# Attention, MoE 1 and MoE 2 on one core: wider staging of MoE 1's weights, nine subtractions moved to VectorE, and new start addresses for split operands

## The chip, the core and the metric

The kernel runs on one core of a Trainium2 chip. A core has TensorE (PE, with its weight loads shown apart as PEld), VectorE (DVE), ScalarE (ACT), GpSimd (POOL) and SyncE (SP), each with its own instruction queue that runs in order, and 16 DMA engines. The metric is the device time of one execution in microseconds; smaller is better.

## The reference

```python
def _attn_ref(q, k, v):                       # (4, 8, 576, 64)
    scores = scale * np.matmul(q, k.transpose(0, 1, 3, 2))
    mask = block_i >= block_j                 # blocks of 64
    scores = np.where(mask, scores, -1000000000.0)
    ...
    return np.matmul(attn, v)                 # softmax in between

def _moe_ref(x, w1, w2, w3, w_out):           # 2304 tokens, 512 -> 1024 -> 512
    a = x @ w1
    b = x @ w2
    h = a * b @ w3
    return h @ w_out

def _moe2_ref(x, w_gate, w_noise, noise, w1, w2):   # 8 experts, top 2
    logits = x @ w_gate
    noisy_logits = logits + np.log1p(np.exp(x @ w_noise)) * noise
    ...
    for e in range(E):
        ...
            h = np.maximum(x[mask] @ w1[e], 0.0)
            out[mask] += top2_w[mask, k, None] * (h @ w2[e])
```

The attention's output, put together over the heads, is the input x of the first MoE, whose output is the input of the second.

## The kernel before

Nearly all products are made of three matmuls (`mm3`, L485 to L487): each operand is split into a high part and a low part in a 32-bit format (`split`, L476 and L480: ACT copies the high part, DVE or POOL subtracts it for the low part), and high x high, high x low and low x high are added up in PSUM. A matmul has a stationary operand, loaded by PEld, and a moving one that streams through the array.

**Attention.** 32 heads (4 batches of 8) run one after the other. Per head, `prep_h` (L604) makes `hi` on ACT (L607, L610), the low half of q on DVE (L609) and `kl`, k's low part, on POOL (L612). `s_unit` multiplies (L639, L642), `s_max` takes the row maxima on DVE (L653) and the exponentials on ACT (L658), `g_unit` transposes (L672) into `pt`, `av_a` and `av_b` multiply with v (L685, L697). The order in which these steps, the conversions and the fillers are recorded is written out by hand in two lists, `FIRST` (L70, for the heads up to number 9) and `LATER` (L71): g, p, a, b, s, h, v and l are steps of heads, `c` is `feed`, `t` a step of the router, `f` lets filler work for PE in. A scheduler then moves instructions within each engine's queue.

**MoE 1's weights.** They arrive as 64-bit numbers. `load64` (L536) fetches a piece of 512 numbers per partition (512 KB in all) into `stg`, which has two buffers; `conv64` (L541) makes 32-bit numbers of it in `stf` with three DVE instructions (L547 to L549), and `feed_half` (L764) splits the piece of the call before into `pc` (L476 on ACT, L480 on DVE), converts the next and issues the load of the one two further on. There are 40 pieces (`w_jobs`, L734). The piece's buffers lie in a pool that stays open as long as the attention.

**MoE 1.** `w_unit` (L717) first multiplies w3 by w_out (64 units of three matmuls, 512 columns wide), so that MoE 1 becomes (x w1 * x w2) w3w_out. After batch 0's heads, `Moe1.steps` (L370) goes over 9 chunks of 256 tokens: `x_load` (L154) fetches the heads' outputs, which were written to DRAM as `x2`, `x_prep` (L185) normalizes and splits them into `x.h` (tile `xh`, L195), `ab` (L199, 8 times a chunk) multiplies 24 times with `xh` as the moving operand, 256 columns, and a piece of w1 or w2 in `pc` as the stationary one; the products' split goes to `gt` (L212). `yout` (L215) multiplies 48 times a chunk with `gt` stationary and `pc` moving, 512 columns. `ab` for unit f waits at recording for the conversions: 28 + 4 * (f // 2) pieces have to be split before. The router (L254) follows each chunk in small steps and keeps its transposed input in `yT`.

**MoE 2.** Per expert, `trans` (L930) makes `xt0` (three blocks of 128 tokens) and `xt1` (two blocks); `ffn1` (L944) multiplies 96 times with `xt` moving (384 columns for `xt0`, 256 for `xt1`) and `pc` stationary; its split goes to `ht0` and `ht1`. `ffn2` (L959) multiplies 24 times for each of the 40 blocks with `ht` stationary and `pc` moving, 512 columns.

## Time and profile before

| | us |
|---|---|
| median of 3 runs | 1100.47 (1100.3 to 1101.81) |
| the profiled execution | 1103.1 |
| its span, first to last instruction | 1101.2 |
| PE busy | 1050.4 |
| DVE busy | 564.4 |
| ACT busy | 494.9 |
| POOL busy | 309.3 |

The profile is of one execution. Busy time counts overlapping instructions of an engine once. A matmul's recorded duration is longer than the distance to the next one, since matmuls are pipelined; what a matmul costs in a row of equal ones is the distance between their starts. The granted TensorE clock (PEclk) is a share of 2.4 GHz and is either 1.0 or 0.5 at any moment; a stretch's figure is the mean.

### The profile page before, as it was taken

The numbers are of one execution on the slowest core, as the hardware profiler recorded it, in microseconds if no ns is written. First come the engines' busy times: TensorE is split into PE (matmuls) and PEld (weight loads), VectorE is DVE, ScalarE is ACT, GpSimd is POOL, SyncE is SP. The second block draws the span as 40 slices with busy tenths as digits, with TensorE's granted clock in tenths as the row PEclk, the third lists the DMA queues.
The fourth block names the chain that finished last, engine by engine and source line by source line (L and its number), as shares of the span: only waits on it lengthen the run. The fifth ranks groups of instructions, "written<-read, shape, count | busy, mean of one in ns | idle before, by whom it ended". The sixth has DMA issues, their size and how long they took to land.

```text
span 1101.2 us, 17515 instructions
## 1 busy us (share of the span) xinstructions
PE 1050.4 (95%) x6588; PEld 941.2 (85%) x6588; DVE 564.4 (51%) x1270; ACT 494.9 (45%) x1180; POOL 309.3 (28%) x315
## 2 busy tenths in 40 slices
PE   4999978999999999999999999999999999999996
PEld 3767767799899999989999889889898989899885
DVE  5988889856665756532454453534333333434111
ACT  5765547666665656422223432433333333333111
POOL 3110122424252242422443325241413222120211
PEclk9999989999999999999999999999999999999999
DMA  9765775325634463322413556563545445351212
GB/s 218 237 199 193 196 200 180 123 79 132 196 96 105 143 156 121 107 68 59 77 40 87 126 106 184 173 163 96 148 102 144 107 125 125 106 115 30 39 20 32
DMA packets 80386, 136.34 MB, mean 124 GB/s; under 512 B 21437, under 2 KB 46757, under 8 KB 80293
## 3 DMA queue, kind: packets, MB, share of 16 engines
q1 hardware_dynamic: 70181, 113.98, 36.4%
q0 software_dynamic: 10112, 21.16, 10.7%
q8 instruction: 54, 0.88, 0.3%
q14 instruction: 39, 0.32, 0.1%
HBM read 103.92 MB, written 31.19 MB: 123 GB/s over the span
## 4 chain that ended last, share of the span: by engine, by line
PE 81%; DMA 8%; DVE 7%; ACT 1%; issue 1%; SPq 1%; POOL 0%; POOLq 0%; DVEq 0%; ACTq 0%
PE ph L485 13%; PE ph L486 13%; PE ph L487 13%; PE m L485 9%; PE m L486 9%; PE m L487 9%; DMA stg<-in_w_dram 4%; PE tp L672 4%; PE av L697 3%; PE sb L642 2%; PE sb L639 2%; PE m L939 1%; DVE stf L549 1%; DVE nm L653 1%; DMA stf<-in_m_dram 1%
## 5 line engine op out<-in xcount | busy, mean ns | idle before, releaser
L485 PE MATMUL m<-xh,pc 128*128 128x256 f32 x576 | 165.2, 290 | 5.6 <-DVE at L211 3.5
L486 PE MATMUL m<-xh,pc 128*128 128x256 f32 x576 | 163.1, 287 | 2.2 <-DVE xh L480 2.2
L487 PE MATMUL m<-xh,pc 128*128 128x256 f32 x576 | 161.2, 287 | 1.9 <-DVE pc L480 1.9
L485 PE MATMUL ph<-xt,pc 128*128 128x384 f32 (+1 forms) x512 | 156.0, 308 | 2.9 <-ACT xt L476 1.6
L486 PE MATMUL ph<-xt,pc 128*128 128x384 f32 (+1 forms) x512 | 157.0, 307 | 0.0
L487 PE MATMUL ph<-xt,pc 128*128 128x384 f32 (+1 forms) x512 | 156.9, 307 | 0.0
L954 DVE SCALAR_TENSOR_TENSOR ht<-ph,ht 128x384 fp32r<-128x384 f32 (+1 forms) x128 | 61.6, 489 | 148.7 <-ACT ht L953 143.5
L480 DVE TENSOR_TENSOR pc<-stf,pc 128x1024 fp32r<-128x1024 f32 (+1 forms) x92 | 92.3, 1016 | 87.2 <-ACT pc L476 83.8
L485 PE MATMUL ph<-pc,ht 128*128 128x512 f32 x320 | 127.8, 400 | 0.0
L486 PE MATMUL ph<-pc,ht 128*128 128x512 f32 x320 | 126.5, 396 | 0.0
L487 PE MATMUL ph<-pc,ht 128*128 128x512 f32 x320 | 126.4, 395 | 0.0
L981 POOL DMA_INDIRECT out_dram<-yo,ids x40 | 64.3, 1606 | 211.5 <-ACT yo L977 124.0
L485 PEld LDWEIGHTS m<-xh,pc 128*128 128x128 f32 x576 | 110.5, 193 | 7.2 <-DVE at L211 3.7
L953 ACT ACTIVATE ht<-ph 128x384 fp32r<-128x384 f32 (+1 forms) x128 | 55.0, 437 | 133.8 <-PE ph L487 127.1
L486 PEld LDWEIGHTS m<-xh,pc 128*128 128x128 f32 x576 | 110.3, 193 | 3.0 <-DVE xh L480 2.6
L487 PEld LDWEIGHTS m<-xh,pc 128*128 128x128 f32 x576 | 109.0, 192 | 2.7 <-DVE pc L480 2.4
L476 ACT CAST pc<-stf 128x1024 fp32r<-128x1024 f32 (+1 forms) x92 | 78.1, 864 | 73.8 <-DVE stf L549 32.5
L658 ACT ACTIVATE pb<-sb,nm 128x288 f32<-128x288 f32 (+3 forms) x192 | 93.5, 496 | 38.4 <-PE tp L672 17.3
L480 POOL TENSOR_TENSOR gt<-at,gt 128x256 fp32r<-128x256 f32 x72 | 57.2, 798 | 183.9 <-ACT gt L476 175.7
L485 PEld LDWEIGHTS ph<-xt,pc 128*128 128x128 f32 x512 | 95.7, 188 | 4.0 <-ACT xt L476 2.1
L612 POOL TENSOR_TENSOR kl<-qk,hi 128x576 fp32r<-128x576 f32 x32 | 47.5, 1484 | 177.2 <-ACT hi L610 136.6
L486 PEld LDWEIGHTS ph<-xt,pc 128*128 128x128 f32 x512 | 96.2, 188 | 0.6 <-DVE xt L480 0.2
(158 smaller groups left out, 2229.0 us busy)
## 6 DMA issues: line engine op xcount, KB each, us to landing
stf<-in_m_dram SPq DMA_DIRECT2D x52, 512.0 KB
qk<-in_qk_dram SPq DMA_DIRECT2D x32, 576.0 KB
stg<-in_w_dram SPq DMA_DIRECT2D x32, 512.0 KB
x<-ev SPq DMA_DIRECT2D x32, 288.0 KB
xab<-x SPq DMA_DIRECT2D x20, 256.0 KB
yt<-y SPq DMA_DIRECT2D x18, 260.0 KB
stg<-in_w_out_dram SPq DMA_DIRECT2D x8, 512.0 KB
v<-in_v_dram SPq DMA_DIRECT2D x24, 160.0 KB
```

The source lines that it names most:

```text
L476: d = nc.scalar.copy(h, src)
L480: return d, eng.tensor_tensor(l, src, r32(h), op=OP.subtract)
L485: nc.tensor.matmul(out, a, c, start=first, stop=False)
L486: nc.tensor.matmul(out, a, d, start=False, stop=False)
L487: nc.tensor.matmul(out, b, c, start=False, stop=last)
L612: nc.gpsimd.tensor_tensor(c.kl, c.qk[:, 1, :], r32(c.hi[:, 1, :]), op=OP.subtract)
L658: nc.scalar.activation(pb[t][:, k0:k0 + src.free_size()], src, AF.Exp, bias=nm, scale=1.0, accum_out=sums[:, h // H, t + n, h % H:h % H + 1])
L672: nc.tensor.transpose(bank[:, n * P:(n + 1) * P], pb[t][:, kt * P:(kt + 1) * P], self.ident)
L697: nc.tensor.matmul(c.av[:, o0:o0 + w], c.vv[:, kt, :], c.pt[:, i, s0:s0 + w], start=(kt == 0 and i == 0), stop=(kt == 4 and i == m - 1))
L953: a = nc.scalar.activation(hh[:, 0, f, :], ph, AF.Relu)
L954: v = nc.vector.scalar_tensor_tensor(hh[:, 1, f, :], ph, 0.0, r32(hh[:, 0, f, :]), op0=OP.max, op1=OP.subtract)
L981: nc.gpsimd.indirect_dma_start(out=self.a["out"], out_offset=self.idx(e, i), in_=yo, in_offset=None, compute_op=OP.add)
```

## The change

1. **Weights in wider pieces.** `stg` and `stf` become 1024 numbers wide, `stg` with two buffers as before and `stf` with one in place of two. `w_jobs` yields 6 pieces of 512 and 17 of 1024 where there were 40 of 512, and `FIRST` has three `c` where it had five. The pool of `stg` and `stf` closes once all pieces are split, and `yT` is put into a pool opened after that.
2. **kl on VectorE.** For heads 0 to 8 the subtraction that makes `kl` is done by DVE; heads 9 to 31 stay on POOL.
3. **Places in SBUF.** The first heads' `pt` lies in the right-hand pool; the first of `gt`'s eight buffers is allocated as soon as its pool opens; `xh` gets 16 numbers (64 bytes) ahead of it; `xt1`'s tile gets 112 numbers behind it; `wv` gets names by the expert's parity in place of two buffers.

Where the tiles begin follows from the two built programs. In bytes of a partition, modulo 512:

| tile | before | after | its part in the matmuls |
|---|---|---|---|
| xh | 384 | 448 | moving, `ab` |
| pc, all 12 | 128 | 128 | stationary in `ab` and `ffn1`, moving in `yout` and `ffn2` |
| gt | 384 | 384 | stationary, `yout` |
| ht0 | 416 | 384 | stationary, `ffn2` |
| ht1 | 448 | 384 | stationary, `ffn2` |
| xt0 | 352 | 352 | moving, `ffn1` |
| xt1 | 448 | 448 | moving, `ffn1` |
| pt, heads 8 to 31 | 480 | 320 | moving, `av` |
| yT | 384 | 448 | moving, router |

Every slice that a matmul takes of these tiles lies a multiple of 512 bytes further on, but for `pt`, where some lie 256 further.

```diff
-FIRST = "g0 g1 t f2.9 c t c o g2 g3 t p s0 t t s1 s2 f2.9 c t a f2.9 t b0 t s3 h t t c c b1 v l"
+FIRST = "g0 g1 t f2.9 c t o g2 g3 t p s0 t t s1 s2 f2.9 c t a f2.9 t b0 t s3 h t t c b1 v l"
...
-            x.h = self.p2b.tile([P, 2, 4, CH], F32R, name="xh")
+            x.h = self.p2b.tile([P, 16 + 8 * CH], F32R, name="xh")[:, 16:].rearrange("p (a t c) -> p a t c", a=2, t=4)
...
-        gt = self.gts[c, f] = self.p2b.tile([P, 2, CH], F32R, name="gt", bufs=8)
+        gt = self.gts[c, f] = self.gt0 if (c, f) == (0, 0) else self.new_gt()
...
-            self.yT = self.p2b.tile([P, 2, 4, CH], F32R, name="yT")
+            self.yT = self.p2c.tile([P, 2, 4, CH], F32R, name="yT")
...
     def load64(self, src, n):
-        t = self.stg.tile([P, 512], I64, name="stg")
+        w = n * src.shape[-1]
+        t = self.stg.tile([P, 1024], I64, name="stg", bufs=2)[:, 0:w]
...
-        f = self.stg.tile([P, 512], F32, name="stf")
+        f = self.stg.tile([P, 1024], F32, name="stf")[:, 0:wi.shape[1]]
...
-                nc.gpsimd.tensor_tensor(c.kl, c.qk[:, 1, :], r32(c.hi[:, 1, :]), op=OP.subtract)
+                (nc.vector if h < NF - 1 else nc.gpsimd).tensor_tensor(c.kl, c.qk[:, 1, :], r32(c.hi[:, 1, :]), op=OP.subtract)
...
-                        c.pt = px.tile([P, 1, PTW], F32, name="pt", bufs=2)
+                        c.pt = pt0[:, h % 2:h % 2 + 1, :]
...
                 for half in range(2):
                     for ft in range(2):
                         yield w3(ft, half * 512)
-                    for g in range(4 * half, 4 * half + 4):
-                        yield wout(g)
+                    if half == 0:
+                        for g in range(2):
+                            yield wout(g)
+                    for g in range(2 + 2 * half, 4 + 4 * half, 2):
+                        yield wout2(g)
                 for ft in range(2, 8):
-                    for o in (0, 512):
-                        yield w3(ft, o)
+                    yield w3(ft, 0, 1024)
                 for m, (n, k, i) in enumerate(W12):
-                    for o in (0, 2):
-                        yield a[n][:, o:o + 2, k * 256:(k + 1) * 256], 2, i, o * 256, 0 if m < 2 else 64
+                    yield a[n][:, :, k * 256:(k + 1) * 256], 4, i, 0, 0 if m < 2 else 64
...
+                if i >= H and moe1.p2c is None and moe1.conv == 40:
+                    stgs.close()
+                    moe1.p2c = moe1.p2s.enter_context(tc.tile_pool(name="p2c", bufs=1, reuse_waits="tile"))
...
-        x = self.xt[e, s] = (self.pa if s == 0 else self.pb).tile([P, 2, 4, n * P], F32R, name=f"xt{s}")
-        wv = self.wv[e, s] = self.pa.tile([P, n], F32, name=f"wv{s}", bufs=2)
+        x = (self.pa if s == 0 else self.pb).tile([P, 8 * n * P + 112 * s], F32R, name=f"xt{s}")
+        x = self.xt[e, s] = x[:, 0:8 * n * P].rearrange("p (m d c) -> p m d c", m=2, d=4)
+        wv = self.wv[e, s] = self.pa.tile([P, n], F32, name=f"wv{s}{e % 2}")
```

VectorE's queue around the eighth head's preparation (`hi` is that head's; `stf` and `stg` are pieces of weights, `nm` row maxima, `ev` a head's output, `tp` and `sb` banks of PSUM). Before:

```order
L547 TENSOR_SCALAR stf_441<-stg_360 128x512
L653 TENSOR_REDUCE nm4_1056<-sb_1050 128x1
L687 COPY ev_1029<-tp_1027 128x128
L548 SCALAR_TENSOR_TENSOR stf_441<-stg_360,stf_441 128x512
L656 TENSOR_REDUCE nm4_1056<-nm4_1056 128x1
L609 SCALAR_TENSOR_TENSOR hi_1186<-qk_1089,hi_1186 64x576
L547 TENSOR_SCALAR stf_449<-stg_401 128x512
L549 SCALAR_TENSOR_TENSOR stf_441<-stg_360,stf_441 128x512
L548 SCALAR_TENSOR_TENSOR stf_449<-stg_401,stf_449 128x512
L653 TENSOR_REDUCE nm0_1137<-sb_1131 128x1
L653 TENSOR_REDUCE nm1_1139<-sb_1131 128x1
L549 SCALAR_TENSOR_TENSOR stf_449<-stg_401,stf_449 128x512
```

With the change:

```order
L553 SCALAR_TENSOR_TENSOR stf_361<-stg_285,stf_361 128x1024
L554 SCALAR_TENSOR_TENSOR stf_361<-stg_285,stf_361 128x1024
L661 TENSOR_REDUCE nm4_941<-sb_935 128x1
L484 TENSOR_TENSOR pc3_70<-stf_361,pc3_70 128x1024
L661 TENSOR_REDUCE nm0_1011<-sb_1005 128x1
L664 TENSOR_REDUCE nm4_941<-nm4_941 128x1
L661 TENSOR_REDUCE nm1_1013<-sb_1005 128x1
L695 COPY ev_910<-tp_908 128x128
L617 SCALAR_TENSOR_TENSOR hi_1069<-qk_966,hi_1069 64x576
L620 TENSOR_TENSOR kl_1073<-qk_966,hi_1069 128x576
L552 TENSOR_SCALAR stf_453<-stg_330 128x1024
L553 SCALAR_TENSOR_TENSOR stf_453<-stg_330,stf_453 128x1024
```

Before, three instructions of pieces 512 wide stand next to the head's `hi` and no `kl`; now `kl` follows `hi` directly, and the two conversions ahead of `hi` are 1024 wide, with the next piece right behind `kl`.

SyncE's queue where chunk 0's x is fetched (`ev` is head 7's output on its way to DRAM, `x2`; `xab` is x's tile; names in brackets are the semaphores it waits for: DMAHW0 to 7 are earlier DMAs, PE the matmuls). Before:

```order
L538 DMA stg_908<-in_w1_dram 128x2x256 [waits DMAHW6_49,DVE_49]
L538 DMA stg_953<-in_w2_dram 128x2x256 [waits DMAHW7_49,DVE_49]
L701 DMA x2_61<-ev_1408 128x576 [waits DMAHW0_49,Activation_49]
L167 DMA xab_1502<-x2_61 64x3x256 [waits DMAHW1_49,PE_49]
L167 DMA xab_1502<-x2_61 64x3x256 [waits DMAHW2_49]
L172 DMA xr_1503<-rs_62 64x3x256 [waits DMAHW3_49,PE_49]
L167 DMA xab_1502<-x2_61 64x3x256 [waits DMAHW4_49]
L167 DMA xab_1502<-x2_61 64x3x256 [waits DMAHW5_49]
L538 DMA stg_961<-in_w2_dram 128x2x256 [waits DMAHW6_49,DVE_49]
```

With the change:

```order
L543 DMA stg_842<-in_w2_dram 128x4x256 [waits DMAHW5_49,DVE_49]
L709 DMA x2_61<-ev_1265 128x576 [waits DMAHW6_49,DVE_49,Activation_49]
L168 DMA xab_1364<-x2_61 64x3x256 [waits DMAHW7_49,DMAHW6_49,PE_49]
L168 DMA xab_1364<-x2_61 64x3x256 [waits DMAHW0_49]
L173 DMA xr_1365<-rs_62 64x3x256 [waits DMAHW1_49]
L168 DMA xab_1364<-x2_61 64x3x256 [waits DMAHW2_49]
L168 DMA xab_1364<-x2_61 64x3x256 [waits DMAHW3_49]
L173 DMA xr_1365<-rs_62 64x3x256 [waits DMAHW4_49]
L543 DMA stg_906<-in_w1_dram 128x4x256 [waits DMAHW5_49,DVE_49]
```

Before, the first read into `xab` waits for its ring and for PE; now it waits also for DMAHW6, which is the write of `ev` just ahead of it, because `xab` lies over the tile that `ev` had.

## Rows read from the trace of the kernel before

**Rows 1.** Part 1 of the page: busy time, share of the span, instructions.

```profile
PE 1050.4 (95%) x6588; PEld 941.2 (85%) x6588; DVE 564.4 (51%) x1270; ACT 494.9 (45%) x1180; POOL 309.3 (28%) x315
```

**Rows 2.** Stretches: us, busy by engine, granted clock, DMA share, GB/s.

```profile
25.00:84.00 59.00, 55.66 (x295) 41.00 (x294) 52.71 (x102) 42.51 (x116) 8.15 (x6) 0.97 0.70 219
84.00:125.00 41.00, 40.20 (x211) 31.79 (x210) 35.64 (x73) 23.04 (x59) 2.85 (x2) 1.00 0.61 202
125.00:160.00 35.00, 27.53 (x172) 24.31 (x171) 27.24 (x51) 17.43 (x46) 7.29 (x6) 0.90 0.79 193
160.00:207.00 47.00, 38.47 (x247) 33.57 (x246) 44.96 (x83) 30.59 (x85) 16.25 (x13) 0.89 0.51 167
...
300.00:470.00 170.00, 169.78 (x1256) 158.84 (x1255) 106.04 (x303) 101.46 (x295) 62.45 (x62) 1.00 0.44 121
...
720.00:1080.00 360.00, 360.00 (x2046) 323.95 (x2045) 114.21 (x168) 118.94 (x197) 83.45 (x79) 1.00 0.42 100
```

**Rows 3.** Timeline of PE: start, duration; first and last matmul of three rows.

```profile
590.60 0.28 PE L485 MATMUL m<-xh,pc 128*128 128x256 f32 x1
...
593.36 0.28 PE L485 MATMUL m<-xh,pc 128*128 128x256 f32 x1
...
821.03 0.28 PE L485 MATMUL ph<-xt,pc 128*128 128x256 f32 x1
...
831.80 0.28 PE L487 MATMUL ph<-xt,pc 128*128 128x256 f32 x1
...
1068.77 0.28 PE L485 MATMUL ph<-xt,pc 128*128 128x256 f32 x1
...
1079.96 0.28 PE L487 MATMUL ph<-xt,pc 128*128 128x256 f32 x1
```

**Rows 4.** Timeline of PE: first and last of a `yout` and of three `ffn2`.

```profile
498.56 0.40 PE L485 MATMUL m<-pc,gt 128*128 128x512 f32 x1
...
509.24 0.40 PE L487 MATMUL m<-pc,gt 128*128 128x512 f32 x1
...
1051.97 0.40 PE L485 MATMUL ph<-pc,ht 128*128 128x512 f32 x1
...
1068.53 0.40 PE L487 MATMUL ph<-pc,ht 128*128 128x512 f32 x1
```

**Rows 5.** Tile stf up to 208 us: count, ns minimum/median/maximum, first and last start.

```profile
L547 DVE TENSOR_SCALAR stf<-stg x40: 406/424/1544, 7.8 to 203.8; 128x512 int32<-128x512 int32 x40
L548 DVE SCALAR_TENSOR_TENSOR stf<-stg,stf x40: 671/683/1874, 9.3 to 205.7; 128x512 int32<-128x512 int32 x40
L480 DVE TENSOR_TENSOR pc<-stf,pc x39: 620/682/2533, 12.2 to 205.1; 128x512 fp32r<-128x512 f32 x39
```

**Rows 6.** DVE's groups by shape: busy us, mean ns, idle before; last row 625:1080.

```profile
L548 DVE SCALAR_TENSOR_TENSOR stf<-stg,stf 128x512 int32<-128x512 int32 x40 | 31.2, 780 | 0.4
...
L480 DVE TENSOR_TENSOR pc<-stf,pc 128x512 fp32r<-128x512 f32 x39 | 29.1, 749 | 0.4 <-ACT pc L476 0.2
L547 DVE TENSOR_SCALAR stf<-stg 128x512 int32<-128x512 int32 x40 | 20.6, 515 | 17.7 <-DMA stg<-in_w_dram 14.9 <-DMA stg<-in_w_out_dram 2.7
L609 DVE SCALAR_TENSOR_TENSOR hi<-qk,hi 64x576 fp32r<-64x576 f32 x15 | 15.2, 1015 | 6.3 <-ACT hi L607 5.8
...
L480 DVE TENSOR_TENSOR pc<-stf,pc 128x1024 fp32r<-128x1024 f32 x52 | 62.5, 1223 | 86.8 <-ACT pc L476 83.7 <-PE ph L487 3.1
```

**Rows 7.** Line 609 up to 208 us: count, ns minimum/median/maximum; who waited for it.

```profile
L609 DVE SCALAR_TENSOR_TENSOR hi<-qk,hi x15: 755/756/1733, 7.0 to 201.5; 64x576 fp32r<-64x576 f32 x15
...
  PE sb L639: 12.9, 4
```

**Rows 8.** POOL's groups up to 208 us, as Rows 6.

```profile
L612 POOL TENSOR_TENSOR kl<-qk,hi 128x576 fp32r<-128x576 f32 x15 | 22.6, 1509 | 106.9 <-ACT hi L610 104.1 <-PE av L697 2.8
L620 POOL TENSOR_TENSOR vv<-v,vv 128x320 fp32r<-128x320 f32 x6 | 7.2, 1200 | 7.8 <-ACT vv L619 7.7
```

**Rows 9.** The chain that ended last, 100 to 210 us: start, us, what.

```profile
145.02 9.55 DMA stg<-in_w_dram
```

More of the change, by code (lines that the diff above doesn't have):

```diff
@@ L555, in attention @@
         moe1 = self.moe1
-        with tc.tile_pool(name="p1", bufs=1, side="right") as p1, tc.tile_pool(name="stg", bufs=2, side="right") as self.stg, \
+        stgs = ExitStack()
+        with tc.tile_pool(name="p1", bufs=1, side="right") as p1, \
                 tc.tile_pool(name="psS", bufs=3, space=PSUM) as psS, \
@@ L566, in attention @@
             sums = p1.tile([P, B, 6, H], F32, name="sums")
+            pt0 = p1.tile([P, 2, PTW], F32, name="pt")
+            self.stg = stgs.enter_context(tc.tile_pool(name="stg", bufs=1, side="right"))
             hd = {}
```

21 lines of the change are left out of this document (14 added, 7 removed).

## The prediction

> **What bounds the kernel now.** I read the page's busy times first, then a table of stretches, then single instructions. PE is busy 1050.4 of 1101.2 us and has 95% of the span; no other engine reaches 52% [rows 1]. The table of stretches says where PE is the limit and where it isn't [rows 2]. From 300 to 470 us PE is busy 169.78 of 170 us while DVE works 106.04; from 720 to 1080 us it is busy 360.00 of 360. There only fewer or shorter matmuls save time. Before 207 us it is otherwise. From 125 to 207 us (two rows) PE is busy 27.53 + 38.47 = 66.0 of 82 us, at a mean granted clock of 0.90 and 0.89, while DVE works 27.24 + 44.96 = 72.2 of 82: here DVE and what feeds it set the pace. From 25 to 125 us PE and DVE are both near full: PE idles 3.3 + 0.8 us, DVE is busy 88.4 of 100. So PE idles 4.1 + 16.0 = 20.1 us from 25 to 207 us. The clock is at half of 2.4 GHz for about 6% of 59, 20% of 35 and 22% of 47 us, some 21 us in all, which costs up to 10 us more. About 30 us can be won in that part at the very most.
>
> The third reading is the distance between starts of matmuls that follow each other without a break, at a granted clock of 1.0. In `ab` 24 matmuls of 256 columns take (593.36 - 590.60) / 23 = 120.0 ns each. In `ffn1` on `xt1`, with as many columns and the same `pc` as stationary operand, 96 take (831.80 - 821.03) / 95 = 113.4 ns in one expert, and (1079.96 - 1068.77) / 95 = 117.8 ns in another [rows 3]. In `yout` 48 matmuls of 512 columns take (509.24 - 498.56) / 47 = 227.2 ns; in `ffn2`, with the same moving tiles and the same width, 72 take (1068.53 - 1051.97) / 71 = 233.2 ns [rows 4]. At 2.4 GHz the columns alone would be 106.7 and 213.3 ns, so each kind pays its own surplus. What differs within each pair is where the split operand begins: `xh` at 384 modulo 512 against `xt1` at 448; `ht0` at 416 (and `ht1` at 448) against `gt` at 384. The change gives `xh` the place of the faster `xt1` and `ht0`, `ht1` that of the faster `gt`.
>
> **The change part by part: places.** `ab` has 9 chunks x 8 x 24 = 1728 matmuls. If they run as `xt1` does, each saves between 120.0 - 117.8 = 2.2 and 120.0 - 113.4 = 6.6 ns: 3.8 to 11.4 us. No row says into which of the two rates a chain of 24 falls, so I take the middle, 4.4 ns and **7.6 us**. Lower bound nothing, if the place isn't the cause. A loss isn't excluded by a row, but the pair that differs in place alone points the other way, and I give it nothing. `ffn2` has 40 x 24 = 960 matmuls; at 227.2 in place of 233.2 ns they save 960 x 6.0 = **5.8 us** (bounds 0 and 5.8). Nearly all of both lie where PE has no idle time [rows 2], so they count in full. `xt0` and `xt1` begin where they did: nothing. `pt` moves from 480 to 320 beside an unmoved `vv`, and `yT` from 384 to 448; for neither is there a row at the new place, and both are few against the 1728: nothing, and 1 us either way in the range. The names of `wv`, the early `gt` buffer and the pools move no work.
>
> The rule that speaks against this: the Trainium skill, "TensorE: Matmul & The Clock Gate", section "Back-to-back issue gap", gives the distance of two matmuls at the full clock as columns / 2.4 + 2.5 ns, with no word on addresses. It would make 109.2 ns of 256 columns wherever they lie; the trace has 113.4, 117.8 and 120.0 for them, so something beside the width counts. By the rule the moves would be worth nothing, which is the first rival below.
>
> **Wider pieces.** A piece of 512 costs DVE 424 (L547), 683 (L548; L549 is of the same form) and 682 ns (L480) at the median [rows 5], 424 + 683 + 683 + 682 = 2472 ns. The split at 1024 takes 1223 ns [rows 6], so 512 numbers more cost 541 ns and the fixed part is some 140 ns. For L548 and L549 the same slope gives 1224. L547 at 424 ns is below that slope already; with half of it, 271 ns, it comes to 695. A wide piece is then 695 + 1224 + 1224 + 1223 = 4366 ns against 2 x 2472 = 4944: 0.58 us less, and 17 x 0.58 = **9.8 us** of DVE. If L547 doubled instead, 17 x 0.42 = 7.2.
>
> **kl on DVE.** This adds nine subtractions 576 long; the nearest row is L609, also 576 long, at 756 ns undisturbed [rows 7]: 9 x 0.756 = 6.8 us of DVE. It takes nine of the 15 from POOL, 9 x 1.509 = 13.6 us of POOL work [rows 8]. While POOL works, DVE's instructions are stretched: L547's mean is 515 against a median of 424, L548's 780 against 683, L480's 749 against 682, L609's 1015 against 756, with single ones up to 2533 [rows 5 to 7]. Mean less median, times the counts, is 3.6 + 3.9 + 2.6 + 3.9 = 14.0 us. POOL's two largest groups in that time are 22.6 (`kl`) and 7.2 us (`vv`) [rows 8]; of these 29.8 the nine have 46%, of all of POOL's work less, and I take 36%: 5 us of stretch goes. Bounds 0, and 13.6 if every moment of them stood in DVE's way. DVE thus gains 9.8 + 5 - 6.8 = 8 us net. Behind `kl` on DVE's queue now stand the next piece's conversion and row maxima; the head's L642 on PE waits for it.
>
> **Fewer, larger loads.** DVE idles 17.7 us ahead of L547 for a piece to land [rows 6], and the chain has a single wait of 9.55 us for such a load [rows 9]. With two buffers a load starts when the conversion two pieces earlier ends. A wide conversion alone covers 695 + 2 x 1224 = 3.1 us where a narrow one covers 1.8, and half as many hand-overs are left; the bytes are the same and the DMA engines are 51 to 79% busy [rows 2]. I let two thirds of the idle time go, 12 us. One buffer for `stf` costs nothing, since the split that frees it stands ahead of the next conversion on the same queue, as the order shows.
>
> **What of it reaches the end.** DVE wins 8 + 12 = 20 us before 207 us. From 25 to 125 us PE has only 4.1 us to give; from 125 to 207 us it idles 16 us and loses clock besides. I count half of the 20: **10 us**, with bounds of -6 (the queue rival below, weakened) and 20. Chunk 0's x now waits for the write of head 7's `ev`: the read that follows could start earlier before. That is one DMA's landing, between nothing and the 9.55 us of the longest wait [rows 9]; since the write was issued just ahead in both orders, and the last quarter of the reads needs it anyway, I take 2 us and leave it inside the 10's bounds.
>
> The sum: 7.6 + 5.8 + 10 = 23.4 us. From the profiled execution's 1103.1 that leaves 1079.7; the median of the runs is 2.6 lower, and from 1100.47 it leaves **1077**.
>
> **The rivals.** (1) Places don't matter; what differs between `ab` and `ffn1` is their neighbours in the queue and in PSUM. Then the 10 us of the first part are all: 1090. (The rule of the Trainium skill's page above would say the same.) For it: `xt1` itself shows two rates at one place. Against: `ab` keeps 120.0 ns at 590 us, when attention has ended. (2) The first part gains nothing, because PE there waits on latencies that a wide piece lengthens as much as it shortens the sum; the places act: 1100.5 - 13.4 = 1087. For it: PE is 98% busy from 84 to 125 us. Against: 16 us of idle PE after that. (3) Slower: DVE's queue. PE waited 12.9 us, four times, for L609 [rows 7]. A head's `hi` and `kl` now stand behind pieces that hold DVE for 4366 ns in place of 2472, and `kl` itself adds 756. If each of the first 12 heads were late by that difference, 1.9 + 0.8 = 2.7 us, PE would lose 32 us; less the 13.4 of the places that is 1119. It decides from 1.1 us a head on, where the loss eats the places' gain. Against: DVE would have to be full at every head, and its load falls. (4) Both act more strongly: 113.4 ns everywhere (11.4), 5.8, and 16 of the 20 us: 33 us, 1067. That the starts aren't where they should be is no rival, since the built program shows them.
>
> **How the numbers follow.** The forecast, 1070 to 1084, has 0.52. Rival 1 (1085 to 1094) 0.14, rival 2 (1084 to 1091) 0.14, rival 4 (1062 to 1070) 0.08, no change because gains and losses meet 0.05, rival 3 0.07. The range reaches from 1066 to 1093 and leaves out the far halves of rivals 1 and 4, no change, and rival 3. A measurement of this kernel can tell 0.2%, 2.2 us, from no change. Faster by more than that: 0.52 + 0.14 + 0.14 + 0.08 = 0.88; the same 0.05; slower 0.07.
>
> **What would show it.** Places: in the timeline late in MoE 1 the starts in `ab` stand 113 to 118 ns apart where they stood 120.0; in `ffn2` 227 in place of 233; `ffn1` and `yout` as they were. Wider pieces: L548's counterpart at 1024 near 1.22 us, 17 times, and less than 6 us of DVE idle for loads. kl: POOL's groups lose nine of them, DVE has nine near 0.76 us, and the means of the conversions come down to their medians. First part: the last conversion ends some 10 us before 207, and PE's idle time from 125 us to there falls below 10 us. The prediction is wrong if `ab` stays at 120 ns or goes above it, or if PE waits longer for a head's `hi` and `kl` than 12.9 us.

## The result, and the profile after

The changed kernel takes 1092.21 us (median; 1087.97 to 1096.28), the kernel before beside it 1101.29. The ratio is 0.9911, 95% interval 0.9892 to 0.9931: 9 to 10 us faster where 23.4 were forecast. Measured again beside other kernels it was 0.9909 (0.9883 to 0.9935). The direction held and the size did not. The time lies inside the forecast's range, 1066 to 1093, by less than 1 us at its upper end, and the wide range is what held it. The profiled execution took 1091.95 us, its span is 1090.1 and the mean granted clock 0.984 (0.988 before).

Part 1 of the page of the changed kernel, the line that answers [rows 1]:

```profile
PE 1042.4 (96%) x6588; PEld 940.8 (86%) x6588; DVE 566.3 (52%) x1211; ACT 494.6 (45%) x1163; POOL 300.5 (28%) x306
```

PE lost 8 us of busy time, and 11.1 us of the span went. So only some 3 us of PE's idle time is gone. The table of stretches of the changed kernel, as [rows 2], says the same of the first part:

```profile
25.00:84.00 59.00, 54.61 (x305) 42.90 (x306) 54.09 (x96) 45.51 (x124) 0.87 (x1) 0.97 0.78 267
84.00:125.00 41.00, 41.00 (x216) 33.08 (x215) 35.57 (x50) 22.39 (x51) 1.88 (x1) 1.00 0.52 173
125.00:160.00 35.00, 27.29 (x165) 23.50 (x163) 26.70 (x39) 17.16 (x46) 10.94 (x8) 0.85 0.78 203
160.00:207.00 47.00, 38.91 (x239) 34.64 (x240) 44.16 (x67) 28.67 (x75) 15.20 (x11) 0.85 0.48 152
...
720.00:1080.00 360.00, 360.00 (x2066) 327.55 (x2063) 111.76 (x164) 118.53 (x197) 82.48 (x79) 1.00 0.40 96
```

From 125 to 207 us PE is busy 27.29 + 38.91 = 66.2 us, where it was 66.0 [rows 2], and the clock is lower (0.85 against 0.90 and 0.89). In the one stretch in which PE had time to give, nothing was won in this execution.

The places acted. The timeline of PE in the changed kernel (start, duration), as [rows 3, 4]: the first and the last of the same 24 matmuls of `ab`, and of the 72 of `ffn2`:

```profile
586.03 0.28 PE L489 MATMUL m<-xh,pc 128*128 128x256 f32 x1
...
588.74 0.28 PE L489 MATMUL m<-xh,pc 128*128 128x256 f32 x1
...
1041.58 0.39 PE L489 MATMUL ph<-pc,ht 128*128 128x512 f32 x1
...
1057.68 0.39 PE L491 MATMUL ph<-pc,ht 128*128 128x512 f32 x1
```

`ab` stands at (588.74 - 586.03) / 23 = 117.8 ns where it stood at 120.0, and `ffn2` at (1057.68 - 1041.58) / 71 = 226.8 where it stood at 233.2.

Where the time went, read from the starts of six matmuls in the two traces (us from the start of the span; the last column is the gain up to there):

```
                               before    changed    gained
last unit of the w3 product     134.3     128.5       5.8
first ab                        136.3     132.8       3.5
first ab of chunk 1             228.1     226.6       1.5
first ab of chunk 5             470.1     464.8       5.3
first ffn2                      642.6     638.1       4.5
last matmul                    1091.0    1079.9      11.1
```

The first part was ahead by 5.8 us at 129 us and by 1.5 us at 227. `ab` and what stands among it brings 3 us up to `ffn2`, and `ffn2` 6.6.

### The profile page after: what moved, and what is told of

The parts are those of the page before. It is cut to its first block, busy times and chain, and to the rows that moved or that the text cites. A ratio compares the mean times of both kernels' runs of the same rounds, so it can differ in the third digit from the quotient of the medians.

```text
span 1090.1 us, 17403 instructions
## 1 busy us (share of the span) xinstructions
PE 1042.4 (96%) x6588; PEld 940.8 (86%) x6588; DVE 566.3 (52%) x1211; ACT 494.6 (45%) x1163; POOL 300.5 (28%) x306
## 4 chain that ended last, share of the span: by engine, by line
PE 78%; DVE 5%; ACT 1%; DMA 1%; issue 1%; POOL 0%; POOLq 0%; ACTq 0%; DVEq 0%
PE ph L489 13%; PE ph L490 13%; PE ph L491 13%; PE m L489 9%; PE m L490 9%; PE m L491 9%; PE tp L680 3%; PE av L705 3%; PE sb L650 2%; PE sb L647 2%; PE m L957 1%; DMA stf<-in_m_dram 1%; DVE hi L617 1%; PE m L247 1%; DVE stf L553 1%
## 5 line engine op out<-in xcount | busy, mean ns | idle before, releaser
L484 DVE TENSOR_TENSOR pc<-stf,pc 128x1024 fp32r<-128x1024 f32 (+1 forms) x75 | 88.1, 1190 | 85.8 <-ACT pc L480 80.5
L489 PE MATMUL ph<-pc,ht 128*128 128x512 f32 x320 | 126.0, 395 | 0.0
L491 PE MATMUL ph<-pc,ht 128*128 128x512 f32 x320 | 124.6, 390 | 0.0
L490 PE MATMUL ph<-pc,ht 128*128 128x512 f32 x320 | 124.5, 390 | 0.0
L484 POOL TENSOR_TENSOR gt<-at,gt 128x256 fp32r<-128x256 f32 x72 | 60.4, 843 | 183.5 <-ACT gt L480 176.6
L480 ACT CAST pc<-stf 128x1024 fp32r<-128x1024 f32 (+1 forms) x75 | 74.8, 1016 | 54.5 <-DMA stf<-in_m_dram 31.6
L489 PEld LDWEIGHTS ph<-xt,pc 128*128 128x128 f32 x512 | 95.8, 188 | 3.4 <-ACT xt L480 2.1
L490 PEld LDWEIGHTS ph<-xt,pc 128*128 128x128 f32 x512 | 96.2, 188 | 0.5 <-DVE xt L484 0.2
L491 PEld LDWEIGHTS ph<-xt,pc 128*128 128x128 f32 x512 | 96.2, 188 | 0.0
```

Source lines behind the costliest of these rows:

```text
L480: d = nc.scalar.copy(h, src)
L484: return d, eng.tensor_tensor(l, src, r32(h), op=OP.subtract)
L489: nc.tensor.matmul(out, a, c, start=first, stop=False)
L490: nc.tensor.matmul(out, a, d, start=False, stop=False)
L491: nc.tensor.matmul(out, b, c, start=False, stop=last)
```

## The experiments

Each ratio is to the kernel before, with its 95% interval; 0.001 is 1.1 us. The changed kernel has 0.991.

### Places: one at a time, and all of them

The kernel before, with `ht` moved alone:

```diff
-        x = self.xt[e, s] = (self.pa if s == 0 else self.pb).tile([P, 2, 4, n * P], F32R, name=f"xt{s}")
-        wv = self.wv[e, s] = self.pa.tile([P, n], F32, name=f"wv{s}", bufs=2)
+        x = (self.pa if s == 0 else self.pb).tile([P, 8 * n * P + 112 * s], F32R, name=f"xt{s}")
+        x = self.xt[e, s] = x[:, 0:8 * n * P].rearrange("p (m d c) -> p m d c", m=2, d=4)
+        wv = self.wv[e, s] = self.pa.tile([P, n], F32, name=f"wv{s}{e % 2}")
```

> The kernel before with one part of the change alone: ht0 and ht1 begin at 384 modulo 512 bytes (they began at 416 and 448); the narrow staging, kl on POOL and xh's place are as before. If the place sets the distance of the matmuls, ffn2's stand 227 ns apart in place of 233.2 and the 960 of them give 5.8 us back: about 1095.5 us where the kernel before has 1101.3, ratio 0.995. If neighbours set it, ffn2 stays at 233 ns and the time at 1101.3.

Measured 1096.41 us, 0.9949 (0.9933 to 0.9966): 5.6 us. The order on every queue is that of before. The timeline of PE in this kernel, first and last of the 72 matmuls of [rows 4]:

```profile
1045.60 0.39 PE L485 MATMUL ph<-pc,ht 128*128 128x512 f32 x1
...
1061.70 0.39 PE L487 MATMUL ph<-pc,ht 128*128 128x512 f32 x1
```

(1061.70 - 1045.60) / 71 = 226.8 ns. The place alone does it, and its 5.8 us reach the end whole.

The kernel before, with the 64 bytes ahead of `xh` alone:

```diff
-            x.h = self.p2b.tile([P, 2, 4, CH], F32R, name="xh")
+            x.h = self.p2b.tile([P, 16 + 8 * CH], F32R, name="xh")[:, 16:].rearrange("p (a t c) -> p a t c", a=2, t=4)
```

> The kernel before with the 64 bytes ahead of xh alone, so that xh begins at 448; behind it in the same pool gt moves from 384 to 448 too, and yT to 448. If places act as the trace of the changed kernel reads: ab at 117.5 ns, 1728 x 2.2 to 2.5 ns = 4 us saved; and yout, whose stationary gt now begins where ht1 began before, takes about 233 in place of 227.2 ns, 432 x 6 = 2.6 us lost. Sum about 1.4 us less than before, within 0.2%. By the forecast's 4.4 ns for ab the saving would be 7.6 and the sum 5 us. If only ffn2's surroundings made its 233 ns, yout stays at 227.2.

Measured 1100.87 us, 0.9986 (0.9974 to 0.9998): 1.5 us, as the sum of a gain and a loss said. In this kernel `ab`'s last three chunks have a mean of 117.7 to 117.8 ns (119.6 to 119.7 with `xh` at 384), and `yout`, whose stationary `gt` was pushed to 448, its first and last of 48 matmuls:

```profile
497.75 0.39 PE L485 MATMUL m<-pc,gt 128*128 128x512 f32 x1
...
508.71 0.41 PE L487 MATMUL m<-pc,gt 128*128 128x512 f32 x1
```

(508.71 - 497.75) / 47 = 233.2 ns, which is `ffn2`'s old number and not `yout`'s 227.2 [rows 4]. One pool, one push of 64 bytes, and a different loop has paid for it.

The changed kernel, with a start that moves on by 64 bytes from chunk to chunk and from expert to expert (one run, 1103.7 us; `yo` has a buffer less, so its time says nothing):

```diff
+            x.h = self.p2b.tile([P, 112 + 8 * CH], F32R, name="xh")[:, 16 * (c % 8):16 * (c % 8) + 8 * CH].rearrange("p (a t c) -> p a t c", a=2, t=4)
...
+        x = (self.pa if s == 0 else self.pb).tile([P, 8 * n * P + 112], F32R, name=f"xt{s}")
+        x = self.xt[e, s] = x[:, 16 * e:16 * e + 8 * n * P].rearrange("p (m d c) -> p m d c", m=2, d=4)
...
+        hh = (self.pa if s == 0 else self.pb).tile([P, 16 * n + 112], F32R, name=f"ht{s}")
+        hh = self.ht[e, s] = hh[:, 16 * e:16 * e + 16 * n].rearrange("p (m f c) -> p m f c", m=2, f=8)
...
-        yo = self.pa.tile([P, DM], F32, name="yo", bufs=3)
+        yo = self.pa.tile([P, DM], F32, name="yo", bufs=2)
```

> A look at places, not a time (yo has two buffers in place of three): the changed kernel where xh begins at (384 + 64 c) modulo 512 in chunk c, xt0 at 480 + 64 e, xt1 at 448 + 64 e, ht0 at 448 + 64 e and ht1 at 384 + 64 e in expert e. If the start modulo 512 sets the distance, the mean distance in ab, ffn1 and ffn2 goes with that start: near 120.0 for xh at 384, 117.5 for xh at 448, 113.4 to 117.8 for xt1 at 448, 227 for ht at 384 and 233 for ht at 416 and 448, and the other starts show whether there is a better one. If neighbours in the queue set it, all chunks and all experts read alike.

The timeline of PE: first and last of 96 matmuls of `ffn1` on `xt1` in experts 3, 6 and 7, where it begins at 128, 320 and 384:

```profile
821.05 0.28 PE L489 MATMUL ph<-xt,pc 128*128 128x256 f32 x1
...
832.43 0.28 PE L491 MATMUL ph<-xt,pc 128*128 128x256 f32 x1
...
995.17 0.28 PE L489 MATMUL ph<-xt,pc 128*128 128x256 f32 x1
...
1006.36 0.28 PE L491 MATMUL ph<-xt,pc 128*128 128x256 f32 x1
...
1069.65 0.28 PE L489 MATMUL ph<-xt,pc 128*128 128x256 f32 x1
...
1081.04 0.28 PE L491 MATMUL ph<-xt,pc 128*128 128x256 f32 x1
```

That is 119.8, 117.8 and 119.9 ns. The mean distance for each start, worked out from all matmuls of that trace at a granted clock of 1.0 that follow each other on the same output (those over 1.15 times the median left out):

```
start modulo 512         0     64    128    192    256    320    384    448
xh  (256 columns)    118.5  115.9  119.0  114.4  119.1  115.9  119.6  117.4
xt1 (256 columns)    119.3  117.8  119.8  117.8  118.7  117.8  119.9  117.8
ht  (stationary)     232.5  229.2  227.8  233.4  232.4  229.1  226.9  233.3
start modulo 512        32     96    160    224    288    352    416    480
xt0 (384 columns)    173.4  173.5  176.7  176.7  173.4  173.5  176.6  176.7
```

`ht` and `xt0` repeat every 256 bytes. Neighbours can't make such a table, so the first rival is out. The two rows of 256 columns are weaker. `xt1` at 448 ran at 113.4 ns in most experts of the kernel before [rows 3], of the changed kernel and of the two runs above, while in this scan 64, 192, 320 and 448 all have 117.8: the second rate at one place is real, and what picks it stays open. Each number for `xh`, but that at 384, is the mean of one chunk and mixes the two rates: the chunk that lies at 192 here, with 114.4 ns, had 116.0 in the changed kernel and 114.2 in the run with the 64 bytes alone, at 448 in both.

The changed kernel with `xh` at 320: `xh` is placed ahead of `gt`, with its 64 bytes behind it, and 64 bytes are saved ahead of both:

```diff
-        cf = p2.tile([P, E + 1], F32, name="cf")
+        cf = p2.tile([P, E + 1], F32, name="no")
...
+                    moe1.xh0 = moe1.new_xh()
                     moe1.gt0 = moe1.new_gt()
```

> The changed kernel with xh at 320 modulo 512 in place of 448 (xh is placed ahead of gt, gt stays at 384, yT goes back to 384). By the scan, where chunk 7 at 320 had a mean of 115.9 ns against 117.7 for that chunk at 448: ab 115.9 ns, 1728 x 1.7 = 3 us less than the changed kernel, 1089. If the mean of 115.9 was the chunk's and not the place's: 117.5 ns and 1092.

Measured 1089.76 us, 0.9895 (0.9874 to 0.9916); `ab`'s mean over the trace is 116.1 ns against 117.4 in the changed kernel, so the scan's 115.9 for this place holds in the mean; the single chunks lie between 114.7 and 117.3. In the kernels further down that have `xh` at 320 too, the mean is 115.2 to 115.4. The time's interval overlaps the changed kernel's.

### The first part by itself

The changed kernel with both places undone:

```diff
-            x.h = self.p2b.tile([P, 16 + 8 * CH], F32R, name="xh")[:, 16:].rearrange("p (a t c) -> p a t c", a=2, t=4)
+            x.h = self.p2b.tile([P, 2, 4, CH], F32R, name="xh")
...
-        x = (self.pa if s == 0 else self.pb).tile([P, 8 * n * P + 112 * s], F32R, name=f"xt{s}")
+        x = self.xt[e, s] = (self.pa if s == 0 else self.pb).tile([P, 2, 4, n * P], F32R, name=f"xt{s}")
...
```

> The changed kernel with both places undone (xh at 384, ht0 at 416, ht1 at 448): the wider pieces and kl on DVE by themselves. By the forecast the first part gives 10 us, so 1091 us with ab at 120 and ffn2 at 233 ns. By the trace of the changed kernel (its rows up to 207 us end no earlier than before's) it gives 0 to 2 us: 1099 to 1101.5. If wide pieces cost time that the places hid, it is above 1103.

Measured 1098.54 us, 0.9961 (0.9942 to 0.9979): 4.3 us (2.3 to 6.4), neither the 10 of the forecast nor the 0 to 2 that the trace of the changed kernel had led me to.

The changed kernel with more work for DVE (`again` holds for the last eight pieces):

```diff
         v.scalar_tensor_tensor(fi, wi[:, :, 1], -0x40000000, fi, op0=OP.bitwise_and, op1=OP.bitwise_or)
+        if again:
+            v.scalar_tensor_tensor(fi, wi[:, :, 1], -0x40000000, fi, op0=OP.bitwise_and, op1=OP.bitwise_or)
```

> The changed kernel with L553 carried out twice for the eight wide pieces of w1 and w2 (the second time changes nothing in the data): 8 x 1.22 = 9.8 us more of DVE, all of it between about 112 and 207 us. Theory D (there DVE's total work sets the pace): the time rises by most of it, 7 to 10 us, to about 1100. Theory W (PE, DVE and ACT stand behind chunk 0's x between 126 and 139 us and what follows has room again): it rises by 0 to 4 us.

Measured 1106.37 us, 1.0039 (1.0017 to 1.0060): 14 us more than the changed kernel for 9.8 us of DVE, more than either branch said. In its trace the first `ab` of chunk 2 starts at 304.2 us against 295.6: 8.6 us are lost in the first part, the rest later. Work added to DVE there costs its full price (the second pass also holds each `stg` buffer longer, which this run can't tell apart). That goes with the forecast's basis, that DVE sets the pace there, and the question is why so little relief arrived.

The changed kernel with chunk 0's L194 behind the next head's `hi`:

```diff
-                    for m in self.marks:
+                    for m in self.marks if c or step != 2 else (self.k.hi,):
...
-                nc.vector.scalar_tensor_tensor(lo, c.qk[64:128, 0, :], 0.125, r32(lo), op0=OP.mult, op1=OP.subtract)
+                self.hi = nc.vector.scalar_tensor_tensor(lo, c.qk[64:128, 0, :], 0.125, r32(lo), op0=OP.mult, op1=OP.subtract)
```

> The changed kernel with chunk 0's multiplication by the sums (L194, two parts) put behind the next head's hi (L617) on DVE's queue, by an order of issue alone; so a head and a piece no longer stand behind the load of x. Theory W: PE's and DVE's idle time between 126 and 139 us (5.9 and 6 us) shrinks and the time falls by 3 to 6 us, to 1086 to 1089. Theory D: nothing changes at the end of the first part, 1092 within 1.5.

Measured 1095.22 us, 0.9929 (0.9902 to 0.9955), no gain, and the time of neither branch. But its first `ab` of chunk 2 starts at 290.1 us, 5.5 us before the changed kernel's 295.6; of chunk 5 at 464.5 against 464.8. In this one trace it was won as expected and lost again at 440 us. DVE's timeline there:

```profile
437.19 5.48 DVE L617 SCALAR_TENSOR_TENSOR hi<-qk,hi 64x576 fp32r<-64x576 f32 x1
```

and POOL's, of the same run:

```profile
436.81 0.74 POOL L484 TENSOR_TENSOR gt<-at,gt 128x256 fp32r<-128x256 f32 x1
437.51 2.36 POOL L191 TENSOR_TENSOR xab<-xab 128x1024 f32<-128x1024 f32 x1
439.84 1.39 POOL L620 TENSOR_TENSOR kl<-qk,hi 128x576 fp32r<-128x576 f32 x1
441.20 0.85 POOL L628 TENSOR_TENSOR vv<-v,vv 128x320 fp32r<-128x320 f32 x1
```

A head's `hi`, 0.756 us undisturbed [rows 7], was held until 0.6 us after the last of four POOL instructions that followed each other without a gap; PE waited 3.3 us for it and then ran at half clock for a while (a mean granted clock of 0.83 from 440 to 450 us). The Trainium skill says in "SBUF — State Buffer", section "SBUF: two separate sides", that DVE and GpSimd share a pair of ports under an exclusive lock, so that the loser is blocked and not slowed. The trace agrees, and here one DVE instruction was passed by three POOL instructions in turn. That isn't always so: in the changed kernel a `hi` at 194.98 us took 2.83 us and ended 0.6 us after the first POOL instruction beside it, though the next one had followed without a gap. What decides is open.

### Pieces, kl and pools

Four kernels with both places as changed and the change's pools tell the two parts apart. The first edit puts `kl` on POOL, the second makes the pieces 512 wide (the other lists of pieces and FIRST likewise as before), the third gives them two buffers of each kind:

```diff
-                (nc.vector if h < NF - 1 else nc.gpsimd).tensor_tensor(c.kl, c.qk[:, 1, :], r32(c.hi[:, 1, :]), op=OP.subtract)
+                nc.gpsimd.tensor_tensor(c.kl, c.qk[:, 1, :], r32(c.hi[:, 1, :]), op=OP.subtract)
```

```diff
-                    yield w3(ft, 0, 1024)
+                    for o in (0, 512):
+                        yield w3(ft, o)
...
```

```diff
-        t = self.stg.tile([P, 1024], I64, name="stg", bufs=2)[:, 0:w]
+        t = self.stg.tile([P, 512], I64, name="stg", bufs=2)[:, 0:w]
...
-        f = self.stg.tile([P, 1024], F32, name="stf")[:, 0:wi.shape[1]]
+        f = self.stg.tile([P, 512], F32, name="stf", bufs=2)[:, 0:wi.shape[1]]
```

> The changed kernel with all kl on POOL again, as before the change; the rest stays. By the forecast's own terms kl cost DVE 6.8 us and took 5 us of stretch away: 1090 to 1094, no difference. If the nine subtractions are harmless because they lie ahead of 81 us, where PE is the limit, the same. If PE's waits for hi and kl (11.7 us after) come from kl on DVE, the time falls by 2 us or more.

> The changed kernel with pieces of 512 in two buffers of 512 for each of stg and stf, as before the change, and all kl on POOL as before; what stays of the change is both places and the pools. If the single stf buffer made the run with narrow pieces slow (1110), this has the places' 9.7 us and nothing else: 1092. If the pools themselves cost something, it is above 1095. If the first part's 4 us came from the pools, 1088.

> As the run with the layout alone, but with kl of the first nine heads on DVE: kl by itself on a sound narrow staging. If kl on DVE is harmless ahead of 81 us, the same time as that run, 1092. If it takes DVE's time from the pieces there, 1094 to 1099. If its 7 us with wide pieces hold here too, 1085.

> The changed kernel with pieces of 512 again (in buffers of 1024 of which half is used), kl on DVE and both places as changed. If the wide pieces give what the run with the first part alone showed, about 4 us, the time rises to 1095 to 1097. By the forecast's terms for them (9.8 us of DVE and 12 us of waits for loads, half of it at the end) it rises by 11, to 1103. If kl on DVE gave those 4 us, it stays at 1092.

```
                        kl on POOL                  kl of 9 heads on DVE
narrow pieces   0.9977 (0.9963 to 0.9991)      1.0066 (1.0038 to 1.0094)
wide pieces     0.9977 (0.9951 to 1.0002)      0.9911 (the changed kernel)
```

Narrow pieces in a single buffer 1024 wide had 1.0073 (1.0049 to 1.0097), so the single buffer isn't what makes the upper right corner slow. Of the expectations one branch held: the layout alone is above 1095, so the pools cost something. With narrow pieces, `kl` on DVE costs some 10 us: there DVE waits 22.2 us between 20 and 125 us for pieces to land (11.1 with `kl` on POOL), and the first `ab` starts at 155 us. With wide ones it gives 7: the write of head 6's `ev` is issued at 95.8 us with `kl` on DVE and at 102.6 with `kl` on POOL. The parts of the change are worth something together that neither has alone. (Wide pieces with `kl` on POOL spread most, 1092.8 to 1104.9 us in ten runs.) Why `kl` on DVE delays the narrow loads isn't shown.

The upper left corner has a finding of its own: with the order of before on every queue, the same staging and both places it has 0.9977 (1098.89 us), where the two places by themselves should come to 0.991 (5.6 us measured for `ht`, 3.8 worked out for `xh`). What is left of the change there is the pools. The issues of SP's queue around the write of head 7's `ev` and the first read of chunk 0's x (start and duration of the issue), first before, then changed:

```profile
121.28 0.34 SPq L701 DMA_DIRECT2D x<-ev  x1
121.72 1.32 SPq L167 DMA_DIRECT2D xab<-x  x2
```

```profile
116.65 0.35 SPq L709 DMA_DIRECT2D x<-ev  x1
121.17 1.29 SPq L168 DMA_DIRECT2D xab<-x  x2
```

Before, the read follows the write by 0.44 us. In the changed kernel head 7 is done 4.6 us earlier, and the read is issued 4.52 us behind its write, 4.1 us more than before: at nearly the old time. The change put `xab` where that `ev` lies (`ev` 152704 to 155008, `xab` 144768 to 152960), so the read waits until the write has landed.

Three kernels more, with `xh` at 320: `xab` and `xr` away from `ev`, by their place ahead of `xh` and `gt`, in the changed kernel and on the narrow staging with `kl` on POOL; and the kernel before with both places and nothing else:

```diff
-        x.ab = self.p2b.tile([P, 4, 2, CH], F32, name="xab")
-        x.r = self.p2b.tile([P, 4, CH], F32, name="xr")
+        x.ab, x.r = self.x0 if c == 0 else self.new_x()
...
+                    moe1.x0 = moe1.new_x()
                     moe1.xh0 = moe1.new_xh()
```

> The changed kernel with xh at 320 and, beside that, xab and xr placed ahead of xh and gt in their pool (at 128320 and 136512), away from head 7's ev (152640 to 154944); the order on every queue is the same. Theory E (the first read of chunk 0's x waits for the write of head 7's ev to land, since the change put xab on its place): the read is issued 0.4 us behind that write in place of 4.8, the first ab starts some 4 us earlier, and the time falls from 1089.8 to 1085 to 1087. Rival (the read's issue is not what ab waits for): 1089.8 within 1.5.

> The run with the layout alone (narrow pieces, kl on POOL, the order of before on every queue) with xh at 320 and xab and xr away from head 7's ev. Theory E: it loses the 5 to 7 us that the pools cost, and 2.6 us more by xh's place: 1089 to 1092 where the layout alone had 1098.9. Rival (the pools cost something else): 1096, by xh's place alone.

> The kernel before with its own pools and staging, and the two places alone: ht0 and ht1 at 384, xh at 320. ffn2 gives 5.7 and ab 1728 x 3.3 = 5.7 us: 1090.5. If places and the first part don't simply add, another time; the difference to e13 is then what wide pieces, kl and the pools are worth when xab is out of the way (4 us by the run with the first part alone, or up to 10 by the forecast).

With the order on every queue unchanged, SP's issues in the first of these are

```profile
118.43 0.35 SPq L715 DMA_DIRECT2D x<-ev  x1
118.88 1.31 SPq L167 DMA_DIRECT2D xab<-x  x2
```

and the wait is gone. It has 1088.21 us, 0.9891 (0.9866 to 0.9917), measured again 1088.98 and 0.9875 (0.9854 to 0.9896), against 1089.76 and 0.9895 with the wait. The read is issued 3.1 us earlier, but POOL, which needs it, starts only 1.1 us earlier (128.59 against 129.71). Up to the first `ab` of chunk 2 the two traces of it gained 1.5 and 0.4 us. So the wait's price is 2 us at most here, not 4; the rival's branch is the nearer one, and the intervals with and without the wait overlap. On the narrow staging without `kl` on DVE (the second run) the same move, and `xh` at 320, bring 0.9977 down to 0.9929 (0.9905 to 0.9953): 5.3 us, between the branches. 2.6 of them were expected of `xh`'s place; by `ab`'s means in the two traces, 117.6 and 115.3 ns, it is 4, and 1 to 3 are left for the wait. So the wait is a part of what the pools cost, and what the rest is isn't shown. The third, the kernel before with the places alone, has 0.9911 (0.9886 to 0.9936): 9.8 us where the expected distances say 11.4 and those of its own trace (`ab` 115.2 ns, against 119.3 in the kernel before) 12.8. Set against the first, wide pieces, `kl` and the pools are worth 2 to 4 us once `xab` is out of the way (0.9891 and 0.9875 against 0.9911, with intervals that overlap); the run with the first part alone said 4.3.

### A version that beats both

`xh` at 320, `xab` and `xr` away from `ev`, and once more chunk 0's multiplication behind the next head's `hi`:

```diff
-                    for m in self.marks:
+                    for m in self.marks if c or step != 2 else (self.k.hi,):
...
```

> As e13 (xh at 320, xab and xr away from ev), and chunk 0's multiplication (L193 there) behind the next head's hi on DVE's queue. If DVE's queue behind x still costs something, the time falls below e13's by 2 to 4 us, to 1084 to 1086; a hi that stands beside POOL's work later can take that back, as in the run with that order alone. If DVE's total is all that counts, e13's time within 1.5 us.

> The kernel of e13 again, beside the changed kernel: ratio 0.988 to 0.990, some 3 us less than the changed kernel (ab at 116.0 in place of 117.6 ns gives 2.7, the read of x ahead of ev's landing 1 to 1.6).

> The changed kernel itself once more, beside the two others of this call: ratio to the kernel before 0.991 within 0.002.

Side by side: changed 0.9909 (0.9883 to 0.9935), without the wait for `ev` 0.9875, and with chunk 0's multiplication moved as well 1087.03 us, 0.9859 (0.9835 to 0.9882), below the changed kernel's interval. The move by itself, 2 us between the last two, isn't clear of their intervals. DVE from 110 to 207 us (us, busy by engine, granted clock) before, changed, and in this last kernel:

```profile
110.00:207.00 97.00, 81.00 (x496) 70.13 (x495) 86.18 (x159) 56.02 (x149) 24.98 (x20) 0.91 0.63 182
```

```profile
110.00:207.00 97.00, 81.19 (x486) 70.83 (x485) 84.25 (x121) 53.13 (x136) 28.01 (x20) 0.88 0.60 173
```

```profile
110.00:207.00 97.00, 83.14 (x521) 72.72 (x521) 90.60 (x130) 57.44 (x149) 30.15 (x21) 0.91 0.64 179
```

The change had left DVE idle 12.75 us where it was idle 10.82; with `xab` away from `ev` it is 8.63, and the last kernel leaves 6.40. One more kernel is the changed one with chunk 0's multiplication moved, and with `kl` of the heads from 15 on put on DVE to keep POOL out of the way:

```diff
-                (nc.vector if h < NF - 1 else nc.gpsimd).tensor_tensor(c.kl, c.qk[:, 1, :], r32(c.hi[:, 1, :]), op=OP.subtract)
+                (nc.vector if h < NF - 1 or h >= 15 else nc.gpsimd).tensor_tensor(c.kl, c.qk[:, 1, :], r32(c.hi[:, 1, :]), op=OP.subtract)
```

> The run with chunk 0's multiplication behind the next head's hi, and kl of the heads from 15 on put on DVE too (they follow 207 us, where DVE works 6 of 10 us); POOL keeps kl of the heads 9 to 14 alone. In that run hi (L617) at 437.19 us took 5.48 in place of 0.76 us while POOL worked without a break to 442.05, and PE waited 3.3 us for it and lost the clock. If POOL's kl makes such waits, they go, the 5 us won by 308 us stay to the end: 1086 to 1089. If not, 1092 to 1095 as that run.

Measured 1091.70 us, 0.9904 (0.9876 to 0.9933). PE is busy 169.43 of 170 us from 300 to 470 where it had lost 3.7, so the stall at 440 us is gone as expected; but its first `ab` of chunk 2 starts at 294.7 us in place of 290.1. In that part PE waits 6.3 us for one `kl` on POOL (6.0 in the run with the move alone) and 7.1 for one `pb` on ACT (3.0 there). No better than the changed kernel.

## Why the prediction was off, point by point

**`ffn2`** was right: 226.8 for a forecast 227.2 ns, and 5.6 us by itself for 5.8.

**`ab`** had the right cause and the wrong size. The step that failed is the choice of the middle, 4.4 ns, between the two rates of `xt1` [rows 3]. `xh` runs in the slower one nearly always: 117.8 ns at 586 us, so 2.2 x 1728 = 3.8 us, the lower bound (by the means over the two traces, 119.3 and 117.4 ns, 3.2 us). Nothing in the rows spoke for the middle. 3.8 of the some 14 us that are missing lie here. `pt` and `yT`, put at nothing, were not tried by themselves.

**The first part** is where the rest is missing. The term was 10 us, the half of 20; by itself it measured 4.3 (2.3 to 6.4). The step that failed is the 20 itself, "DVE wins 8 + 12 = 20 us before 207 us". From 25 to 207 us DVE is busy 160.52 us where it was 160.55 [rows 2], and idle 21.5 where it was 21.4; the stretch reaches only 1.5 us further into the work, by the first `ab` of chunk 1. PE idles 15.8 us from 125 to 207 us, where the forecast's sign asked for less than 10. Its parts one by one:

- *Wide pieces, the duration*: a piece was put at 4366 ns. DVE's groups of the pieces between 110 and 207 us, before (busy us, mean ns, idle ahead):

```profile
L548 DVE SCALAR_TENSOR_TENSOR stf<-stg,stf 128x512 int32<-128x512 int32 x18 | 14.9, 830 | 0.0
L480 DVE TENSOR_TENSOR pc<-stf,pc 128x512 fp32r<-128x512 f32 x18 | 14.9, 828 | 0.0
...
L549 DVE SCALAR_TENSOR_TENSOR stf<-stg,stf 128x512 int32<-128x512 int32 x17 | 13.2, 778 | 0.1
...
L547 DVE TENSOR_SCALAR stf<-stg 128x512 int32<-128x512 int32 x17 | 7.7, 451 | 8.5 <-DMA stg<-in_w_dram 8.5
```

  and after:

```profile
L553 DVE SCALAR_TENSOR_TENSOR stf<-stg,stf 128x1024 int32<-128x1024 int32 x9 | 14.9, 1655 | 0.2
...
L484 DVE TENSOR_TENSOR pc<-stf,pc 128x1024 fp32r<-128x1024 f32 x9 | 11.8, 1311 | 1.6 <-ACT pc L480 1.5
L554 DVE SCALAR_TENSOR_TENSOR stf<-stg,stf 128x1024 int32<-128x1024 int32 x9 | 11.6, 1292 | 0.1
...
L552 DVE TENSOR_SCALAR stf<-stg 128x1024 int32<-128x1024 int32 x8 | 6.7, 835 | 0.1
```

  The undisturbed instructions are 684, 1217, 1217 and 1215 ns (medians over all 23 pieces, 17 of them wide), 4333 together: right as durations. What they cost was mis-sized, since DVE's recorded durations overlap like a matmul's. DVE's timeline (start, duration) where instructions follow without a gap, before:

```profile
133.22 0.68 DVE L480 TENSOR_TENSOR pc<-stf,pc 128x512 fp32r<-128x512 f32 x1
133.82 0.68 DVE L548 SCALAR_TENSOR_TENSOR stf<-stg,stf 128x512 int32<-128x512 int32 x1
134.42 0.95 DVE L193 TENSOR_TENSOR xr<-xab,xr 128x768 f32<-128x768 f32 x1
```

  and after:

```profile
147.79 1.22 DVE L554 SCALAR_TENSOR_TENSOR stf<-stg,stf 128x1024 int32<-128x1024 int32 x1
148.93 0.75 DVE L212 TENSOR_TENSOR at<-at,m 128x256 f32<-128x256 f32 x2
```

  An instruction of 0.68 us is followed after 0.60, one of 1.22 after 1.14. The medians of such distances up to 208 us are 341 ns (L547) and three times 602 for a piece of 512, and 599 and three times 1134 for one of 1024: 4294 ns for two narrow pieces, 4001 for a wide one. So a wide piece saves 0.29 us and not 0.58, and 17 of them 5.0 us and not 9.8. Beside that, only eight of the 17 and a part of a ninth lie after 110 us, where DVE sets the pace; there the pieces' durations come to 45.0 us in place of 50.7. The others lie where PE is the limit, and the forecast counted them at the same rate.
- *kl*: nine at 751 ns, 6.8 us as said (6.0 by the distances of 668 ns), all of them begun ahead of 81 us. So POOL's relief lies there too: after 110 us POOL works 28.01 us in place of 24.98, and L553 is stretched to a mean of 1655 ns. The 5 us of stretch that should have gone did not go where they count.
- *The waits for loads* fell from 17.6 to 6.9 us up to 208 us, nearly the 12 that were booked, but others came. What DVE waited for from 110 to 207 us (engine, tile and line, for whom: us, times, longest), before:

```profile
DVE stf L547 <- DMA stg<-in_w_dram: 8.5, 4, 4.3
DVE nm L653 <- PE sb L642: 1.8, 3, 0.7
```

  after:

```profile
DVE xr L194 <- POOL xab L191: 5.2, 2, 4.6
DVE nm L661 <- PE sb L650: 3.0, 4, 1.2
DVE pc L484 <- ACT pc L480: 1.5, 2, 1.1
DVE at L212 <- ACT at L211: 1.4, 2, 1.1
...
```

  and in the kernel that beats both:

```profile
DVE at L212 <- ACT at L211: 1.6, 2, 1.3
DVE pc L490 <- ACT pc L486: 1.5, 2, 1.1
...
DVE xr L193 <- POOL xab L190: 0.6, 1, 0.6
```

  This is where the forecast failed most: 12 us of idle time were booked as won, with no look at what stands next in the queue once a load is no longer late. The largest of it was chunk 0's x. DVE got to L194 at 126.3 us, before POOL had xab (129.05 to 130.86), and everything behind L194 stood 4.57 us. Taking L194 out of the way, and `xab` away from `ev`, is worth 5 us side by side with the changed kernel; 3.6 of them are `xh`'s place if `ab`'s means in the two traces count (117.4 and 115.3 ns), so less than 2 us are left for the queue's order, and no run shows them clear of the intervals.
- *One buffer for `stf` costs nothing* was wrong by little: DVE's waits for ACT's copy ahead of the split rose from 0.2 to 3.1 us between 25 and 207 us.
- *Chunk 0's x waits for the write of head 7's `ev`* was named and put at 2 us. The wait is 4.1 us long, and its price 2 at most.

**The rivals.** The first (places don't matter) fell to the scan, though the time lies in its range, 1085 to 1094. The second (the first part gains nothing, the places act) is nearest to what happened, with `ab` at its lower bound. The third (DVE's queue holds `hi` back) did not come: PE's waits for `hi` are 11.7 us, three of them, for 12.9 in four [rows 7]. The fourth is out.

**What stays open.** 5.6, 3.8 and 4.3 us add up to 13.7, and the change has 10. Each interval is about 2 us wide to either side, and the places by themselves fell 1.6 to 3 us short of their own sum too; whether the parts get in each other's way or this is the measurement's width can't be told. The changed kernel's times spread over 8.3 us, those before over 2.6 in the same comparison; that goes roughly with the mean clock (0.987 at 1087.97 us, 0.981 at 1096.28, but 0.980 at 1092.57), and what makes the clock differ between executions of one program was not found. What the pools cost beside the wait, and which of its two rates a row of 256-column matmuls takes, are open as well.

## What to carry to other kernels

A relief is worth what is left of it in the stretch where that engine is the limit: count the instructions there, not over the whole first half, price them by the distance between their starts and not by their recorded durations, and read what the engine stands on next in its queue before an idle time is booked as won. When tiles are moved, list whose place each one takes and until when that tenant's last DMA runs; an exchange of places is a new wait. And where one operand's start matters, move it with everything that stands behind it in its pool in view: here 64 bytes for one loop were paid by another.
